# The up-projection's second half as rows: y of three token blocks made token by token, their gate logits as dot products on VectorE, and w_out's gated transpose in sixteen pieces

## The chip, the cores and the metric

The kernel runs on one core of one Trainium2 chip. The time is device microseconds of one launch; the span is the part of it that the profile covers.

## The reference

Three layers follow one another on 1536 tokens of 512 features:

```python
# 1: attention of 16 heads, keys masked by a 6-bit hash (head_dim 64, 768 tokens)
x = attention(q, k, v, proj)                       # (1536, 512)
# 2: one dense layer pair, called MoE1 here
h = x @ w_in                                       # 512 -> 2048
g = np.maximum(h, 0.0) + alpha * np.minimum(h, 0.0)
y = g @ w_out                                      # 2048 -> 512
# 3: eight experts, each with room for 192 tokens
logits = y @ w_gate                                # (1536, 8)
# the largest logit of all picks first, until every token has an expert with room
for e in range(8):
    out[mask_e] = np.maximum(y[mask_e] @ w1[e], 0.0) @ w2[e]
```

Since the choice of experts hangs on an order among 12288 logits, y and the logits are made to nearly fp32 accuracy: a product of two fp32 matrices is three fp32r products of their high and low parts.

## The kernel before

All is one instruction stream for each engine, written out by a planner (`Plan`): each operation (`op`) names the engines it may run on with a cost in us, a wished time `at`, what it follows, and which buffers it takes and gives back; a list scheduler then fixes engine and order. So a changed cost or wished time moves instructions everywhere, though they compute the same. The constants at the head of the file (`XP`, `RP`, `XA`, `RD`, ...) are such times.

In MoE1 the tokens are four blocks of 384 (blk 0 to 3) and the 2048 features are 16 groups f of 128.

- **h** (L699 to L701): for each f 12 fp32r products of 384 columns on TensorE (PE) into `psh`; then ScalarE (ACT) makes two parts (a1 L718, a2 L720), VectorE (DVE) joins them to `gt` (a3, L722), ACT takes the high part `gh` (L926), and DVE or GpSimd (POOL) the low part `gl` (`lo`, L930).
- **y** (L728 to L730): two feature groups later, 12 fp32r products of 384 columns for each f into `psy`. w_out is the stationary operand, so y comes out transposed: four banks of 128 features x 384 tokens.
- **End of a block** (blk 0 to 2): four copies `out` of y into `yt`; on PE four products with the gate matrix in column groups (`logit`, L798), a copy, three small products that add the groups (`pick`, L734), and four 128x128 transposes for each of three token groups t (`y_rows`, L777), whose rows `ysb` are stored to DRAM for the experts' gathers.
- **Block 3** takes its logits from g directly, with `wog` = w_out times w_gate, made while blocks 0 to 2 run (`wog_ops`): for each of four quarters q, four loads of w_out transposed, three DVE turns each that undo the 8-byte layout (L849, L851, L853), four products of 512 columns in four column groups (`prod`, L858), a copy, four small products (`add`, L866). Its h stage comes first; its y follows while the routing starts.
- **Conversions:** during block 0 w_out and the rest of w_in arrive as 8-byte numbers. DVE puts each piece together in three steps (L602, L605, L608), ACT takes the high part (L613), DVE the low part (L614). DVE also makes the low parts `xl` of the next block's input (L672), which may go to POOL where its op says so.
- **Experts:** h of an expert is `pl` (L1439), its output is split in 128 tokens (`oa`, L1471) and 64 tokens (`ob`, L1465); the gathered inputs are transposed by L1413 and L1414; routing's products (`rp`) lie between.

Of the kernel before, what the change touches and what calls it, by code (L numbers as in the profile page):

```python
# [7 lines left out]
F32 = mybir.dt.float32  # L8
# [16 lines left out]
XP = 10.89  # L25
RP = 11.53
RB = 19.57
PK0 = -119.54
PK = -106.32
# [8 lines left out]
WA = -6.05  # L38
XA = -32.34
TA = 20.0  # L40
TB = 1.5
YA = 0.74
RD = 2.82
# [4 lines left out]
IA = -7.85  # L48
# [480 lines left out]
class Moe:  # L529
    def __init__(s, tc, ctx, ident, w_in, w_out, w_out_t, alpha, w_gate, w1, w2, out):  # L530
        s.tc, s.nc, s.ident = tc, tc.nc, ident
        s.w_in, s.w_out, s.w_out_t, s.alpha, s.w_gate, s.w1, s.w2, s.out = w_in, w_out, w_out_t, alpha, w_gate, w1, w2, out
# [128 lines left out]
    def x_ops(s, pl, blk, k, after, at, w, take=()):  # L661
# [12 lines left out]
        o = pl.op({"ACT": 0.41}, hi, at, after, take)  # L674
        return pl.op({"DVE": 0.47, "POOL": 0.96} if blk else {"DVE": 0.47}, lambda e="DVE": lo(e), at + 0.4 * w, [o])
# [71 lines left out]
    def moe1(s, pl, r):  # L747
# [47 lines left out]
        def logit(blk):  # L795
            ps = T["lp", blk] = s.bank("pst", "OB")
            for k in range(4):
                nc.tensor.matmul(ps[32 * k:32 * k + 32, 0:NB], s.wg[:, k, :], T["yt", blk, k], start=True, stop=True)  # L798

# [4 lines left out]
        def logitp(blk):  # L804
            T["p2", blk] = s.bank("pst", "OB")
            s.pick(T["lt"], T["p2", blk])
# [7 lines left out]
        def y_after(blk):  # L814

            at = (blk * 16 + 15 + LAG) * U + 2.0
            o_o = []
# [20 lines left out]
        def wog_ops():  # L838
            raw = s.xT[:, :, 512:768].bitcast(U32)
            two = raw.rearrange("p a (n two) -> p a n two", two=2)  # L840
            src = s.w_out_t.rearrange("(p k) f -> k p f", k=4)

            def load(q, k):
                nc.sync.dma_start(out=raw, in_=src[k][:, q * 512:q * 512 + 512].bitcast(U32).rearrange("p (a n) -> p a n", a=4))

            def turn(k, n):
                t = s.xT[:, k, 0:512].bitcast(U32).rearrange("p (a n) -> p a n", a=4)
# [24 lines left out]
            for q in range(4):  # L872
                o_t = []
                for k in range(4):
                    at = (TA + (4 * q + k) * TB) * U
                    o_l = op({"SP": 0.45}, lambda q=q, k=k: load(q, k), at - 2 * U, o_x[1], ["RAW"], dma=1.46)
                    for n, t in enumerate((0.34, 0.6, 0.6)):
                        o_l = op({"DVE": t}, lambda k=k, n=n: turn(k, n), at + 0.1 * n, [o_l] + o, (), ["RAW"] if n == 2 else [])
                    o_t.append(o_l)
                a = op({"PE": 0.9}, prod, at + 0.5, o_t, ["OB"])  # L880
                a = op({"ACT": 0.5}, prodc, at + 0.6, [a], (), ["OB"])
                a = op({"PE": 0.8}, add, at + 0.7, [a], ["OB"])
# [13 lines left out]
        o_y, o_L, o_s, o_wog = {}, [], [], {}  # L896
# [3 lines left out]
        for blk in range(4):  # L900
            if blk < 3:
# [689 lines left out]
```

## Time and profile before

| | |
|---|---|
| median of 3 runs | 739.23 us (738.7 to 740.27) |
| profiled execution | 736.62 us |
| its span | 734.5 us |
| PE busy | 709.9 us, 97% of the span |
| DVE busy | 448.9 us, 61% |
| ACT busy | 311.3 us, 42% |
| POOL busy | 257.7 us, 35% |
| mean granted clock of PE | 0.991 |

The profiled execution took 2.1 us more than its span, and 2.6 us less than the median of the timed runs. Attention fills the first 226 us of the span; MoE1's blocks 0 to 2 end near 306, 380 and 454 us, block 3's h stage at 490, its y at 534; then come the experts to about 727 us and the last scatter.

### The profile page before, as it was taken

What the parts mean: (1) busy time and instruction counts of PE and PEld (TensorE: products, weight loads), DVE (VectorE), ACT (ScalarE), POOL (GpSimd) and SP (SyncE); (2) the same over time, 40 slices, a digit from 0 to 9 for tenths busy, and PEclk for the clock granted to TensorE, in tenths of its full rate; (3) what the DMA queues carried; (4) which work ended last, traced back from release to release, by engine and by line L of the source; (5) the groups of instructions that cost most, each with busy time, mean ns of one, the idle gap of its engine ahead of it and who ended that gap; (6) DMA issues with size and microseconds to landing.
All of it is one profiled execution on the core that took longest, in us unless ns stands there. A gap on an engine that the chain in (4) does not pass through costs nothing. (4 is left out here: it accounts for less than half of the span.)

```text
span 734.5 us, 14803 instructions
## 1 busy us (share of the span) xinstructions
PE 709.9 (97%) x6062; PEld 602.2 (82%) x6062; DVE 448.9 (61%) x989; ACT 311.3 (42%) x569; POOL 257.7 (35%) x220
## 2 busy tenths in 40 slices
PE   7999999999988799999999999999999999999996
PEld 6888888888887699999999999898978667666662
DVE  4888988888976989724454533456667565551000
ACT  4677787778743444633353333541021111112110
POOL 2498888889761121100000000005243413323101
PEclk9999999999999999999999999999999999999999
DMA  8455665655205455130223200200667546539201
GB/s 226 99 138 139 152 172 131 175 138 138 45 2 172 141 174 174 37 97 29 87 65 127 86 1 1 76 2 1 217 256 296 220 174 231 200 144 376 98 7 37
DMA packets 33091, 93.27 MB, mean 127 GB/s; under 512 B 4448, under 2 KB 17920, under 8 KB 30720
## 3 DMA queue, kind: packets, MB, share of 16 engines
q1 hardware_dynamic: 28016, 52.08, 24.8%
q0 software_dynamic: 4688, 39.85, 14.8%
q8 instruction: 48, 0.79, 0.4%
q10 hardware_dynamic: 320, 0.40, 0.2%
q14 instruction: 19, 0.16, 0.1%
HBM read 71.86 MB, written 8.65 MB: 110 GB/s over the span
## 5 line engine op out<-in xcount | busy, mean ns | idle before, releaser
L440 POOL TENSOR_TENSOR pl<-p 128x768 f16<-128x768 f32 (+1 forms) x94 | 134.5, 1449 | 35.6 <-ACT p L432 35.4
L334 DVE TENSOR_REDUCE m<-psm 128x1 bf16<-128x768 f32 x96 | 89.8, 956 | 13.9 <-PE psm L328 12.5
L432 ACT ACTIVATE p<-pss 128x768 f32<-128x768 f32 (+1 forms) x98 | 76.4, 797 | 40.2 <-PE pss L426 30.9
L699 PE MATMUL psh<-xh,win 128*128 128x384 f32 x256 | 87.9, 343 | 1.6 <-ACT xT L505 0.9
L701 PE MATMUL psh<-xh,win 128*128 128x384 f32 x256 | 85.9, 335 | 0.0
L700 PE MATMUL psh<-xl,win 128*128 128x384 f32 x256 | 85.7, 335 | 0.0
L930 POOL TENSOR_TENSOR gl<-gt,gh 128x384 fp32r<-128x384 f32 x18 | 19.1, 1066 | 171.4 <-ACT gh L926 169.7
L729 PE MATMUL psy<-gh,wout 128*128 128x384 f32 x192 | 65.2, 340 | 2.8 <-DVE wout L614 2.8
L728 PE MATMUL psy<-gl,wout 128*128 128x384 f32 x192 | 65.9, 343 | 2.0 <-ACT wout L613 2.0
L451 PE MATMUL av<-v,pl 128*128 128x65 f16 x576 | 63.5, 195 | 2.4 <-DVE xt L489 2.4
L730 PE MATMUL psy<-gh,wout 128*128 128x384 f32 x192 | 65.0, 338 | 0.0
L1471 PE MATMUL oa<-xw,ht 128*128 128x512 f32 x128 | 64.7, 598 | 0.0
L722 DVE SCALAR_TENSOR_TENSOR gt<-psh,al,gt 128x384 f32<-128x384 f32 x48 | 29.5, 615 | 55.4 <-ACT psh L720 55.3
L451 PEld LDWEIGHTS <-pl 128*128 128x128 f16 x576 | 53.9, 100 | 11.1 <-issue 11.0
L452 PE MATMUL av<-v,p 128*128 128x65 f16 x576 | 63.1, 195 | 0.0
L453 PE MATMUL av<-v,p 128*128 128x64 f16 x576 | 62.8, 195 | 0.0
L1439 PEld LDWEIGHTS pl<-xg,xw 128*128 128x128 f32 x256 | 42.1, 190 | 19.0 <-issue 18.2
L718 ACT ACTIVATE gt<-psh 128x384 f32<-128x384 f32 x48 | 23.6, 492 | 78.7 <-PE psh L701 78.7
L1439 PEld LDWEIGHTS pl<-xT,xw 128*128 128x128 f32 x256 | 41.9, 190 | 16.8 <-issue 14.6
L424 PE MATMUL pss<-Q,K 128*128 128x384 f32 x192 | 54.8, 364 | 0.9 <-ACT p L432 0.8
L699 PEld LDWEIGHTS psh<-xh,win 128*128 128x128 f32 x256 | 48.1, 188 | 8.2 <-issue 6.1
L452 PEld LDWEIGHTS <-p 128*128 128x128 bf16 x576 | 54.1, 99 | 0.1
(237 smaller groups left out, 1660.8 us busy)
## 6 DMA issues: line engine op xcount, KB each, us to landing
K<-Q SPq DMA_DIRECT2D x45, 192.0 KB, 2.9
wraw<-in_moe_w_out_dram SPq DMA_DIRECT2D x16, 512.0 KB, 3.6
xT<-in_moe_w_out_t_dram SPq DMA_DIRECT2D x16, 512.0 KB, 3.6
wraw<-in_moe_w_in_dram SPq DMA_DIRECT2D x12, 512.0 KB, 4.4
vf<-in_v_dram SPq DMA_DIRECT2D x16, 192.0 KB, 4.2
qk<-in_q_dram SPq DMA_DIRECT2D x15, 192.0 KB, 3.3
qk<-in_k_dram SPq DMA_DIRECT2D x15, 192.0 KB, 3.5
Q<-Q SPq DMA_DIRECT2D x15, 192.0 KB, 3.8
```

The costliest lines, as they stand in the source:

```text
L334: nc.vector.tensor_reduce(T["m"][:, t:t + 1], T["mx", t][:, :, 0:384], axis=AX.XY, op=OP.max, negate=True)
L432: nc.scalar.activation(T["p", c].rearrange("p (a n) -> p a n", a=2)[:, x], T["s", c][:, x, 0:384], AF.Exp, scale=0.125)
L440: (nc.vector if eng == "DVE" else nc.gpsimd).tensor_tensor(T["l", c][:, x], p[:, x], T["h", c][:, x], op=OP.subtract)
L451: nc.tensor.matmul(o[:, t, 0:65], lo[:, sl], vt[:, 0:65], start=(c == 0 and t == 0), stop=False, **kw)
L452: nc.tensor.matmul(o[:, t, 0:65], ph[:, sl], vt[:, 0:65], start=False, stop=False, **kw)
L699: nc.tensor.matmul(o, wl[:, k, ff], s.xh[blk][:, k], start=(k == 0), stop=False)
L700: nc.tensor.matmul(o, wh[:, k, ff], s.xl[blk][:, k], start=False, stop=False)
L701: nc.tensor.matmul(o, wh[:, k, ff], s.xh[blk][:, k], start=False, stop=(k == 3))
L728: nc.tensor.matmul(o, wh, gl, start=first, stop=False, skip_group_check=True)
L729: nc.tensor.matmul(o, wl, gh, start=False, stop=False, skip_group_check=True)
L730: nc.tensor.matmul(o, wh, gh, start=False, stop=last, skip_group_check=True)
L1439: nc.tensor.matmul(T["h", j // 2][:, j % 2], w1[:, k, j * 128:(j + 1) * 128], T["xg"][:, k], start=(k == 0 and j % 2 == 0), stop=(k == 3), ...
```

## The change

**y as rows.** In blocks 0 to 2 g is now the stationary operand: for each f and each 128 tokens t, three fp32r products with 512 columns of w_out (`yr`, `yr_mm`), 9 for each f and three banks instead of 12 and four. The rows are copied from `psy` to `ysb` and stored; `out`, `logit`, `pick` and `y_rows` are gone there.

**Logits.** For each row tile, 8 instructions on DVE (`dots`): ysb times a gate row broadcast over the partitions, with the sum taken into a column of `L` by the instruction's accumulator. There are 72, spread over the block that follows (`DA`). The gate rows come by three broadcast loads (`gate_rows`) behind the input of block 1 in `xT`'s room and in a tile of its own.

**wog.** The transposed w_out is handled in 16 pieces of 128 features instead of 4 quarters of 512 for each k: one load of all four k, the three turns, then `prod` with four products of 128 columns. The turns wait for a buffer `WT`; the first load waits for the input of block 2 instead of block 1, and a1 of block 3 stands behind the last piece.

**Planner.** Costs and wished times change with it, so that the order moves in all of MoE1 and the experts.

```diff
-XP = 10.89
...
-XA = -32.34
...
-RD = 2.82
+XP = 27.665
...
+XA = 60.587
...
+RD = 30.33
...
-        return pl.op({"DVE": 0.47, "POOL": 0.96} if blk else {"DVE": 0.47}, lambda e="DVE": lo(e), at + 0.4 * w, [o])
+        return pl.op({"DVE": 0.54, "POOL": 1.1} if blk else {"DVE": 0.54}, lambda e="DVE": lo(e), at + 0.4 * w, [o])
...
+    def yr_mm(s, o, f, t, gh, gl, first, last):
+
+        nc = s.nc
+        tt = slice(t * 128, t * 128 + 128)
+        wh, wl = s.wo_part(f, 0), s.wo_part(f, 1)
+        nc.tensor.matmul(o, gl[:, tt], wh, start=first, stop=False, skip_group_check=True)
+        nc.tensor.matmul(o, gh[:, tt], wl, start=False, stop=False, skip_group_check=True)
+        nc.tensor.matmul(o, gh[:, tt], wh, start=False, stop=last, skip_group_check=True)
...
-        def y_rows(blk, t):
-            T["p", blk, t] = s.bank("pst", "OB")
-            for k in range(4):
-                nc.tensor.transpose(T["p", blk, t][:, k * 128:(k + 1) * 128], T["yt", blk, k][:, t * 128:(t + 1) * 128], s.ident)
...
+            nc.sync.dma_start(out=d, in_=s.gate_t[:, e0 * 512:(e0 + n) * 512].to_broadcast([128, n * 512]).rearrange("p (e d) -> p e d", e=d.shape[1]))
...
-            any_copy(e, T["r", blk, t], T["p", blk, t])
+            any_copy(e, T["r", blk, t], T["y", blk, t])
+
+        def dots(blk, t, e):
+            like = lambda x: x.rearrange("p (a d) -> p a d", a=s.wgb[e].shape[1])
+            nc.vector.scalar_tensor_tensor(like(s.junk[:, 0:512]), like(T["r", blk, t]), 1.0, s.wgb[e], op0=OP.mult, op1=OP.mult,
+                                           accum_out=s.L[:, blk * 3 + t, e:e + 1])
...
-            for k in range(4):
-                o_o.append(op({"ACT": 0.37, "DVE": 0.47}, lambda e, k=k: out(e, blk, k), at, [o_y[blk, 15, k]], ["WR"] if k % 2 == 0 else [], ["L"],
-                              o_o[-1:]))
-            at += YA
-            o_l = op({"PE": 0.65}, lambda: logit(blk), at, o_o, ["OB"])
...
+                for e in range(8):
+                    o = op({"DVE": 0.78}, lambda t=t, e=e: dots(blk, t, e), at + DA * (8 * t + e), [o, o_gate[max(e // 2 - 1, 0)]], (), (["T"] + (["WR", "WR"] if blk == t == 2 else [])) if e == 7 else [], [a])
+                o_L.append(o)
...
-                for k in range(4):
-                    nc.tensor.matmul(T["wp"][32 * k:32 * k + 32], s.wg[:, k, :], s.xT[:, k, 0:512], start=True, stop=True)
+                    nc.tensor.matmul(T["wp"][32 * k:32 * k + 32, c * 128:c * 128 + 128], s.wg[:, k, :], w[:, k], start=True, stop=True)
...
-                o_gl = op({"DVE": 0.85, "POOL": 1.0}, lo, at + 1.3, [o], (), ["GT"] if b else [])
+                o_gl = op({"DVE": 0.55, "POOL": 1.1}, lo, at + 1.3, [o], (), ["GT"] if b else [])
...
-                        o_y[blk, f, k] = op({"PE": 0.49}, lambda blk=blk, f=f, k=k: y(blk, f, k), at + 0.1 * k,
+                        o_y[blk, f, t] = op({"PE": 0.68}, lambda blk=blk, f=f, t=t: yr(blk, f, t), at + 0.1 * t,
```

On PE, the end of a block before (here block 0, while block 1 begins): the rows from `pick` to the first transposes.

```order
L734 MATMUL pst<-c,lt 128x8 x3
L728 MATMUL psy<-gl,wout_4582 128x384
L729 MATMUL psy<-gh,wout_4582 128x384
L730 MATMUL psy<-gh,wout_4582 128x384
L728 MATMUL psy<-gl,wout_4582 128x384
L729 MATMUL psy<-gh,wout_4582 128x384
L730 MATMUL psy<-gh,wout_4582 128x384
L777 MATMUL pst<-c,yt 128x128 x4
```

The four gate products L798 stand seven rows ahead of these, and two more transposes L777 x4 behind, each after six products of 384 columns. In the changed kernel the last y products of block 0 (L738 to L740, w_out's last quarter) stand directly ahead of block 1's h (L700 to L702).

```order
L738 MATMUL psy<-wout_4585,gl 128x512
L739 MATMUL psy<-wout_4585,gh 128x512
L740 MATMUL psy<-wout_4585,gh 128x512
L700 MATMUL psh<-xh,win_76 128x384
L701 MATMUL psh<-xl,win_76 128x384
L702 MATMUL psh<-xh,win_76 128x384
L700 MATMUL psh<-xh,win_76 128x384
```

So nothing is left on PE between the blocks. On DVE, early in block 0 of the kernel before, the low parts of block 1's input (L672) stand ahead of the low part of w_out's second quarter (L614, `wout_4583`).

```order
L608 SCALAR_TENSOR_TENSOR pscv<-wraw,pscv 128x512
L672 TENSOR_TENSOR xl<-xT,xh 128x384
L602 TENSOR_SCALAR pscv<-wraw 128x512
L672 TENSOR_TENSOR xl<-xT,xh 128x384 x3
L614 TENSOR_TENSOR wout_4583<-pscv,wout_4583 128x512
```

The changed kernel has the same place without them; a low part of g (L954) stands two rows behind the L615 of that quarter, and one more stands further ahead.

```order
L609 SCALAR_TENSOR_TENSOR pscv<-wraw,pscv 128x512
L603 TENSOR_SCALAR pscv<-wraw 128x512
L723 SCALAR_TENSOR_TENSOR gt<-psh,al,gt 128x384
L615 TENSOR_TENSOR wout_4583<-pscv,wout_4583 128x512
L606 SCALAR_TENSOR_TENSOR pscv<-wraw,pscv 128x512
L954 TENSOR_TENSOR gl<-gt,gh 128x384
```

The four L672 of block 1 moved to POOL, and the low parts of g of some feature groups came from POOL to DVE. In block 3's h stage DVE now has dots (L805) between the a3 (L723) and the low parts (L954).

```order
L723 SCALAR_TENSOR_TENSOR xT<-psh,al,xT 128x384
L805 SCALAR_TENSOR_TENSOR junk,L<-ysb,wgb 128x512
L805 SCALAR_TENSOR_TENSOR junk,L<-ysb,xT 128x512
L954 TENSOR_TENSOR win_77<-xT,win_77 128x384
L723 SCALAR_TENSOR_TENSOR xT<-psh,al,xT 128x384
L805 SCALAR_TENSOR_TENSOR junk,L<-ysb,xT 128x512
L954 TENSOR_TENSOR win_78<-xT,win_78 128x384
```

The kernel before has only L722 and L930 there. On PE in the experts, before, the 64-token tails L1465 of expert 5 stand in parts between the h of expert 6 (L1439).

```order
L1465 MATMUL ob<-xw_5_8617,ht 64x512 x2
L1439 MATMUL pl<-xT,xw_6_8782 128x192 x7
L1465 MATMUL ob<-xw_5_8617,ht 64x512 x2
L1439 MATMUL pl<-xT,xw_6_8782 128x192 x3
L1471 MATMUL oa<-xw_5_8617,ht 128x512
L1439 MATMUL pl<-xT,xw_6_8782 128x192 x2
```

After, expert 5 stands in whole runs (h L1463, tails L1489, mains L1495).

```order
L1463 MATMUL pl<-xg,xw_5_8351 128x192 x30
L1489 MATMUL ob<-xw_5_8495,ht 64x512 x8
L1495 MATMUL oa<-xw_5_8495,ht 128x512 x8
L1437 MATMUL pl<-c,xT 128x128
L1438 MATMUL pl<-c,xT 128x128
```

Over all eight experts the 64 tail products stood in 26 runs, and stand in 12 now.

## Rows read from the trace of the kernel before

**Rows 1.** Windows by stage: busy us (instructions) of each engine, granted clock, DMA.
```profile
226.00:306.00 80.00, 74.49 (x413) 72.79 (x411) 70.64 (x117) 39.83 (x85) 16.66 (x16) 0.98 0.45 143
306.00:380.50 74.50, 74.50 (x451) 71.03 (x450) 32.58 (x59) 28.69 (x62) 1.24 (x1) 1.00 0.21 66
454.20:490.40 36.20, 36.20 (x228) 31.95 (x228) 19.12 (x43) 20.29 (x47) 1.07 (x1) 1.00 0.11 39
```

**Rows 2.** Timeline of PE, end of block 0: start, busy us, instruction.
```profile
305.77 0.34 PE L701 MATMUL psh<-xh,win 128*128 128x384 f32 x1
306.04 0.85 PE L798 MATMUL pst<-yt,wg 128*32 128x384 f32 x8
...
309.74 0.60 PE L777 MATMUL pst<-c,yt 128*128 128x128 f32 x4
...
314.22 0.34 PE L728 MATMUL psy<-gl,wout 128*128 128x384 f32 x1
...
316.31 0.34 PE L699 MATMUL psh<-xh,win 128*128 128x384 f32 x1
```

**Rows 3.** Timeline of PE, experts.
```profile
605.65 1.02 PE L1471 MATMUL oa<-xw,ht 128*128 128x512 f32 x2
606.50 0.49 PE L1439 MATMUL pl<-xg,xw 128*128 128x192 f32 x2
606.83 0.44 PE L1315 MATMUL rp<-tt,xT 128*128 128x2 f16 x12
```

**Rows 4.** Timeline of PE, one `prod` of `wog`, and a product in column groups of attention.
```profile
397.69 1.07 PE L858 MATMUL pswg<-xT,wg 128*32 128x512 f32 x8
398.69 0.45 PE L728 MATMUL psy<-gl,wout 128*128 128x384 f32 x1
398.97 0.34 PE L729 MATMUL psy<-gh,wout 128*128 128x384 f32 x1
...
69.58 0.53 PE L281 MATMUL psz<-qk,pz 128*32 128x192 f32 x8
70.05 0.62 PE L328 MATMUL psm<-K,Q 128*128 128x384 f32 x2
```

**Rows 5.** Timeline of PE, block 0, in brackets the idle time before.
```profile
255.05 0.41 PE L728 MATMUL psy<-gl,wout 128*128 128x384 f32 x1 [1.23 <-ACT wout L613]
257.50 0.66 PE L729 MATMUL psy<-gh,wout 128*128 128x384 f32 x1 [2.04 <-DVE wout L614]
...
258.27 0.52 PE L728 MATMUL psy<-gl,wout 128*128 128x384 f32 x1
258.59 0.52 PE L729 MATMUL psy<-gh,wout 128*128 128x384 f32 x1
```

**Rows 6.** Timeline of DVE, the same stretch.
```profile
255.34 1.50 DVE L672 TENSOR_TENSOR xl<-xT,xh 128x384 fp32r<-128x384 f32 x3
256.76 0.68 DVE L614 TENSOR_TENSOR wout<-pscv,wout 128x512 fp32r<-128x512 f32 x1
257.36 0.69 DVE L605 SCALAR_TENSOR_TENSOR pscv<-wraw,pscv 128x512 uint32<-128x512 uint32 x1
```

**Rows 7.** Timeline of PE, tails of one expert between the next expert's h.
```profile
694.68 1.08 PE L1465 MATMUL ob<-xw,ht 128*64 128x512 f32 x4
695.69 0.92 PE L1439 MATMUL pl<-xg,xw 128*128 128x192 f32 x4
696.53 1.08 PE L1465 MATMUL ob<-xw,ht 128*64 128x512 f32 x4
```

**Rows 8.** Timeline of DVE, attention: two fp32 sources in SBUF.
```profile
9.89 1.02 DVE L273 SCALAR_TENSOR_TENSOR K<-K,c,kk 128x768 fp32r<-128x768 f32 x1
10.83 1.01 DVE L273 SCALAR_TENSOR_TENSOR Q<-Q,c,qq 128x768 fp32r<-128x768 f32 x1
```

**Rows 9.** Timeline of ACT, attention: an accumulator read.
```profile
16.65 0.19 ACT L365 ACTIVATION_READ_ACCUMULATOR vabs<-vf 128x1 f32 x1
16.87 0.53 ACT L365 ACTIVATE vabs<-vf 128x384 bf16<-128x384 f32 x1
```

More of the change, by code (lines that the diff above doesn't have):

```diff
@@ L24 @@
 XWAIT = 0.0005
-XP = 10.89
[L26 to L29, printed above, removed]
+XP = 27.665
+RP = 3.994
+RB = 52.305
+PK0 = 38.012
+PK = 16.878
 NPL = 4
@@ L37 @@
 LAG = 2
-WA = -6.05
-XA = -32.34
-TA = 20.0
-TB = 1.5
-YA = 0.74
-RD = 2.82
+WA = -4.451
+XA = 60.587
+TA = 22.847
+DA = 4.774
+TB = 1.087
+YA = -3.908
+RD = 30.33
 HC = 1
@@ L529, with __init__ @@
 class Moe:
-    def __init__(s, tc, ctx, ident, w_in, w_out, w_out_t, alpha, w_gate, w1, w2, out):
+    def __init__(s, tc, ctx, ident, w_in, w_out, w_out_t, gate_t, alpha, w_gate, w1, w2, out):
         s.tc, s.nc, s.ident = tc, tc.nc, ident
-        s.w_in, s.w_out, s.w_out_t, s.alpha, s.w_gate, s.w1, s.w2, s.out = w_in, w_out, w_out_t, alpha, w_gate, w1, w2, out
+        s.w_in, s.w_out, s.w_out_t, s.gate_t, s.alpha, s.w_gate, s.w1, s.w2, s.out = w_in, w_out, w_out_t, gate_t, alpha, w_gate, w1, w2, out
         s.ctx = ctx
@@ L672, in lo @@
             (nc.vector if e == "DVE" else nc.gpsimd).tensor_tensor(s.xl[blk][:, k], s.xT[:, k, n], s.xh[blk][:, k].bitcast(F32), op=OP.subtract)
-        o = pl.op({"ACT": 0.41}, hi, at, after, take)
-        return pl.op({"DVE": 0.47, "POOL": 0.96} if blk else {"DVE": 0.47}, lambda e="DVE": lo(e), at + 0.4 * w, [o])
+        o = pl.op({"ACT": 0.5}, hi, at, after, take)
+        return pl.op({"DVE": 0.54, "POOL": 1.1} if blk else {"DVE": 0.54}, lambda e="DVE": lo(e), at + 0.4 * w, [o])
     def x_init(s, cl):
@@ L802, in logitc, with yr @@
             any_copy(e, T["lt"], x()[:, 0:NB])
-        def logitp(blk):
-            T["p2", blk] = s.bank("pst", "OB")
-            s.pick(T["lt"], T["p2", blk])
+        def yr(blk, f, t):
+            if f == 0:
+                T["y", blk, t] = s.bank("psy", "L")
+            g = s.g[blk, f]
+            s.yr_mm(T["y", blk, t], f, t, g[1], g[2], f == 0, f == 15)
         def y(blk, f, k):
@@ L838, in wog_ops, with load, turn @@
         def wog_ops():
-            raw = s.xT[:, :, 512:768].bitcast(U32)
+            raw = s.xT[:, :, 768:1024].bitcast(U32)
             two = raw.rearrange("p a (n two) -> p a n two", two=2)
[L841 to L847, printed above, removed]
+            w = s.xT[:, :, 1024:1152]
+            src = s.w_out_t.rearrange("(p k) f -> p k f", k=4)
+            def load(q, c):
+                f = (4 * q + c) * 128
+                nc.sync.dma_start(out=raw, in_=src[:, :, f:f + 128].bitcast(U32))
+            def turn(n):
+                t = w.bitcast(U32)
                 if n == 0:
@@ L875, in wog_ops @@
                     at = (TA + (4 * q + k) * TB) * U
[L876 to L882, printed above, removed]
+                    o_l = op({"SP": 0.45}, lambda q=q, k=k: load(q, k), at - 2 * U, o_x[2], ["RAW"], dma=1.46)
+                    for n, t in enumerate((0.45, 0.7, 0.75)):
+                        o_l = op({"DVE": t}, lambda n=n: turn(n), at + 0.1 * n, [o_l], ["WT"] if n == 0 else [], ["RAW"] if n == 2 else [])
+                    o_t.append(op({"PE": 0.35}, lambda k=k: prod(k), at + 0.5, [o_l], ["OB"] if k == 0 else [], ["WT"]))
+                o_wt.extend(o_t)
+                a = op({"ACT": 0.5}, prodc, at + 0.6, o_t, ["T"], ["OB"])
+                a = op({"PE": 0.8}, add, at + 0.7, [a], ["OB"], ["T"])
                 o = [op({"DVE": 0.1}, lambda q=q: addc(q), at + 0.8, [a], (), ["OB"])]
@@ L894, in sel @@
             s.pick(T["lt"], s.p, False)
-        o_y, o_L, o_s, o_wog = {}, [], [], {}
+        o_y, o_L, o_s, o_wog, o_wt = {}, [], [], {}, []
+        s.wgb = {}
+        o_x[1] = x_block(1)
+        o_x1 = o_x[1]
+        o_gate = [op({"SP": 0.6}, lambda i=i: gate_rows(i), 8 * U, o_x1, (), dma=3.2 - 1.6 * i) for i in range(2)]
+        o_gate.append(op({"SP": 0.6}, lambda: gate_rows(2), 12 * U, (), ["WR", "WR"], behind=[o_w[15]], dma=1.6))
         o_h = []
@@ L900, in moe1 @@
         for blk in range(4):
-            if blk < 3:
+            if blk < 3 and blk + 1 not in o_x:
                 o_x[blk + 1] = x_block(blk + 1)
@@ L1525, in body @@
     ident = c[:, 0:128]
-    m = Moe(tc, ctx, ident, w_in, w_out, w_out_t, alpha, w_gate, w1, w2, out)
+    m = Moe(tc, ctx, ident, w_in, w_out, w_out_t, gate_t, alpha, w_gate, w1, w2, out)
     m.sel = c[:, 260:268]
```

65 lines of the change are left out of this document (36 added, 29 removed).

## The prediction

> **What bounds it now.** I read the windows by stage first: from 226 us on PE is busy in nearly all of each stage, 74.5 of 74.5 us in block 1 [rows 1]. So in MoE1 and the experts an edit is worth what it takes off PE, unless another engine then comes late. Two stages have another engine near: in block 0 DVE is busy 70.6 of 80 us, and PE idles 5.5 us; in block 3's h stage DVE is busy 19.1 of 36.2 us [rows 1]. In block 1 DVE has some 40 us free, and block 2 repeats it. The timelines then give what each removed, added or moved piece costs on PE, and in block 0 what it waits for. Time is accounted against the profiled run, 736.6 us (2.1 us above its span, 2.6 us under the median).
>
> **Ends of blocks.** From the L701 at 305.77 to the L728 at 314.22 there are 8.45 us, with 31 products of 384 columns in them [rows 2]. Twelve such products, from 314.22 to 316.31, take 2.09 us, so 0.174 each [rows 2], and 31 take 5.40. The 3.05 us left are the logit, pick and three transposes with their edges. They go in three blocks, on PE, which is the path: **-9.1 us**. The row copies stay, reading `psy` instead of `pst`; two of three banks must be free when the next block's y begins, over 4 us of h later, so they cost nothing.
>
> **y as rows.** 192 products of 384 columns take 33.4 us a block. 144 products of 512 do the same columns in fewer instructions, and no row has that form. Bounds: if time goes by columns alone, 0.174 x 512/384 = 0.232 us each, 33.4 us, no gain. At the other end, L1471 needs 0.85 us for two records of 512 columns, 0.427 each [rows 3]; L1439's record of 192 takes 0.165 [rows 3], 0.86 ns a column against 0.45 for fp32r, so a record is about two fp32r passes and a pass of 512 takes 0.214: 30.8 us, -2.6 a block, -7.8 in all. Between them: at the low clock the y product takes 0.32 us (258.27 to 258.59) [rows 5], at the high one 0.174; a part that doubles with the clock (0.146) and one that does not (0.028) give 0.195 + 0.028 = 0.223 us for 512. That is also the middle, and I take it: 144 x 0.223 = 32.1, -1.3 a block, **-3.9 us** (0 to -7.8).
>
> **wog in pieces.** A `prod` of four 512-column products takes 1.00 us to the next product, and four of 192 columns in column groups 0.47 [rows 4]. On a line through both, 128 columns take 0.15 + 0.21 = 0.36 us. The product behind takes 0.1 more than its 0.174 (398.69 to 398.97 [rows 4]), and I give the edge ahead as much, so 0.2 for both: 4 x 1.20 = 4.8 before, 16 x 0.56 = 9.0 after, **+4.2 us**. Lower bound +3.2 (edges do not repeat wholly), upper +5.5 (all of 0.47 plus edges). The turns have the same elements on DVE, now in blocks 1 and 2, where it has room; a late turn would hold PE at a piece, but the pieces are spread over two blocks.
>
> **Block 0.** PE idles 1.23 us for ACT's high part of w_out and then 2.04 us for DVE's low part (L614) [rows 5]. DVE is not idle: ahead of that L614 stand three xl, 1.42 us from 255.34 to 256.76, 0.47 each, and one more before [rows 6]. The four go to POOL, 1.9 us off DVE; one a3 and one low part more come ahead of this L614, about 1.0. What is late next is the conversion itself: it comes 0.9 us earlier. PE also ran at half its clock after the wait, at 0.32 instead of 0.174 us a product [rows 5], for eleven products: 1.6 us. With a shorter wait that may or may not happen, so I count half: **-1.7 us**. Bounds 0 (another piece of the chain is as late) and -4.9 (both waits and the low clock go). POOL has room (16.7 of 80 us busy [rows 1]) for the four.
>
> **Experts.** Four tail records of 64 tokens take 1.01 us to the next h [rows 7], where four passes of 0.214 would be 0.86; the four records of h behind them take 0.84 [rows 7] instead of 4 x 0.165 = 0.66. A change to the 64-row form and back thus costs about 0.35 us. The order has 26 such runs before and 12 after: 14 x 0.35 = **-4.9 us** (0 if the cost sits in the instructions, not in the change).
> Whole runs of one expert leave PE nothing to do between its h and its output where ht, a gather or a weight is late. Before, the mains of the expert before lay there. I take **+1.0 us** for such waits (0 to 3 in the likeliest case).
>
> **The dots.** 72 instructions of 128x512 with two fp32 sources in SBUF and an accumulator, DVE only. No row has all of this. DVE starts a 512-element instruction every 0.60 us (256.76 to 257.36) [rows 6]; two fp32 SBUF sources of 768 elements take 0.94 us (9.89 to 10.83) [rows 8], no slower per element; the one accumulator read in rows is ACT's, 0.22 us (16.65 to 16.87) [rows 9]. So 0.60 to 0.82 us; I take 0.78, nearer the upper, since each also waits for the one before. In blocks 1 and 2 24 x 0.78 = 19 us hide in 40 us of room. The tight place is block 3's h stage, where the a3 frees the bank of h: 36.2 us less 3.0 of block end is 33.2 us. DVE's 19.1 us in 43 instructions [rows 1] hold about 0.08 each of overlap (busy 0.68, next start after 0.60 [rows 6]), so 15.7 us of occupancy; one row copy goes from it, but 0.6 us pass before the first dot has its row. That leaves 33.2 - 15.7 - 0.6 = 16.9 us. Two of the 24 dots stand behind the last a3; 22 x 0.78 = 17.2, 0.3 us too long; since a3s also fall behind a dot now and then, I add 0.9: **+1.2 us** (0 at 0.60, +2.0 at 0.82).
> The DMAs are three broadcast loads, 2 MB, behind the conversion's loads, and sixteen of w_out transposed as before; block 1 moves 66 GB/s at a DMA share of 0.21 [rows 1], so they are hidden.
>
> **Sum.** -9.1 - 3.9 + 4.2 - 1.7 - 4.9 + 1.0 + 1.2 = -13.2 us: 723.4 us for the profiled run, 726.0 for the median.
>
> **Rivals.**
> 1. *DVE paces block 3 (slower).* If a dot with an accumulator runs at half the rate of a plain instruction, its 512 elements take twice the 0.94 x 512/768 = 0.63 us, 1.25, and with an accumulator read of 0.22, 1.47 us. Then 22 x 1.47 - 16.9 + 0.9 = 16.3 us are lost in block 3 instead of 1.2: -13.2 - 1.2 + 16.3 = +1.9, 741.1 us. It eats the whole gain (14.4 without this term) from 0.04 us less, d = 1.38. Against it: rows 8's full rate with two such sources. For it: no row has the accumulator. The Trainium skill, "Vector Engine (DVE) Microarchitecture Reference", "Points that are easy to get wrong", says that this instruction with two non-bf16 SBUF sources runs at half throughput, both read ports being taken and none left for the accumulator's readback. By that rule the trace disagrees for the form without an accumulator (0.94 us for 768), and no run here shows the form with one. Chance 0.08.
> 2. *The experts take it back.* Each of eight changes of expert, and the routing phases that now stand denser in the first half, wait 1 to 2 us for ht, a gather or weights: 10 us more, 736 us (731 to 740). For it: PE has at most two banks of h ahead and no mains to fill in. Against it: h of one expert comes in eight chunks, so only the last one's ht is new when the tails begin, and the mains stand behind the tails. Chance 0.13.
> 3. *Cheap rows.* The 512-column product takes 0.214 us: 3.9 us more gain, 722.1 us. For it: L1471's records carry almost no fixed part [rows 3]. The Trainium skill, "TensorE: Matmul & The Clock Gate", gives N/2.4 + 2.5 ns for the isolated gap, 216 ns at N = 512; by that y would come to 144 x 0.216 = 31.1 us a block, -6.9 in all, where 384 columns by the same rule would be 0.1625 and the trace has 0.174. Chance 0.15.
> 4. *Grouping and block 0 give nothing* (-6.6 missing): 732.6 us. The form's cost would have to sit in the instruction, which the slower h records behind a tail [rows 7] speak against. Chance 0.10, inside the range.
>
> **From chances to numbers.** The forecast as summed has 0.54 (723 to 730), rivals as given. The range from 721 to 737 leaves out rival 1, the upper part of rival 2 and the outer edge of rival 3, about 0.17. 0.2% (1.5 us) is what a measurement of this kernel can tell. Faster by more: all but rival 1 and a quarter of rival 2, and a rest for a mechanism not seen: 0.86; within: 0.06; slower: 0.08.
>
> **What would show it.** Right: PE without a gap at 306, 380 and 454 us, L738 to L740 starting every 0.223 us, L805 every 0.6 to 0.8 us, PE's wait for L615 near 256 us shorter, and tails at 0.22 us a record. Wrong: waits of h (L700) for a3 (L723) in block 3's stage over 2 us; low clock in a stage that had none; waits at L1489 or L1463 for ht or xg; pieces L876 waiting for their turns. The weakest terms are the form of the y product, since no row has it, and the experts' order.

## The result, and the profile after

The changed kernel took 727.87 us (median of 4, 725.68 to 728.81) beside 739.75 before: 0.9841 of the time before, 95% interval 0.9813 to 0.9869. A second set of runs gave 725.57 us and 0.9847 (0.9825 to 0.9869). So some 11.5 us are gone; 13.2 were forecast, 726.0 us for the median.

The windows by stage of the changed kernel (first profile; columns as in [rows 1]), cut at the first h of MoE1, the ends of the three blocks, the first y product behind block 3's h and the first h of the experts:

```profile
226.59:305.27 78.68, 75.31 (x360) 67.21 (x361) 67.24 (x110) 38.58 (x80) 13.16 (x13) 0.96 0.47 151
305.27:377.12 71.85, 71.85 (x401) 62.05 (x399) 50.18 (x108) 26.19 (x57) 3.83 (x3) 1.00 0.24 79
377.12:451.00 73.88, 73.88 (x425) 63.47 (x425) 48.57 (x101) 24.44 (x54) 7.58 (x6) 1.00 0.24 78
451.00:486.33 35.33, 35.33 (x218) 31.82 (x216) 30.23 (x80) 19.98 (x46) 4.11 (x7) 1.00 0.10 37
486.33:529.74 43.41, 42.15 (x340) 38.67 (x339) 30.42 (x111) 5.11 (x12) 17.79 (x17) 1.00 0.28 93
529.74:727.00 197.26, 189.82 (x1185) 131.83 (x1182) 84.08 (x321) 31.00 (x61) 53.92 (x47) 0.99 0.51 190
```

In blocks 1 to 3 PE is busy all the time: DVE went from 32 to 50 us in block 1 [rows 1] and from 19 to 30 in block 3's h stage, and PE waits for it nowhere there. The second profile has the same lengths but for block 0:

```profile
225.13:301.14 76.01, 72.50 (x361) 64.54 (x361) 67.19 (x110) 38.54 (x80) 13.19 (x13) 1.00 0.48 157
```

The 2.7 us between the two are the granted clock at the start of MoE1. In the first profile of the changed kernel (timeline of PE) the first 18 products start 0.32 us apart, until 232.4 us: the granted clock is 0.5 there, the lower of TensorE's two levels, after PE had waited 1.83 and 0.90 us at attention's end.

```profile
227.08 0.53 PE L701 MATMUL psh<-xl,win 128*128 128x384 f32 x1
227.40 0.53 PE L702 MATMUL psh<-xh,win 128*128 128x384 f32 x1
```

in the second one 0.17 us apart:

```profile
225.42 0.34 PE L701 MATMUL psh<-xl,win 128*128 128x384 f32 x1
225.59 0.33 PE L702 MATMUL psh<-xh,win 128*128 128x384 f32 x1
```

This low clock falls in some executions of the changed kernel and of the edited forms of the kernel before, and not in others, so a stage's length is compared below between profiles alike in it. By the timelines, from the start of a stage's first product to that of the next stage's, in us ("early" is a low clock at MoE1's start; block 3 is its h stage, y(3) what follows it):

| profile | early | block 0 | block 1 | block 2 | block 3 | y(3) | experts to end |
|---|---|---|---|---|---|---|---|
| before | no | 79.25 | 74.02 | 74.05 | 36.90 | 44.06 | 200.74 |
| changed, first | yes | 78.45 | 71.85 | 73.88 | 34.80 | 44.17 | 197.26 |
| changed, second | no | 75.78 | 71.85 | 73.88 | 34.79 | 44.18 | 197.29 |
| second less before | | -3.5 | -2.2 | -0.2 | -2.1 | +0.1 | -3.4 |

(The first four columns go from last y to last y, block 3's to its last h.) That adds up to -11.3 us, and -0.3 in attention, which no instruction of PE changed: the span of 734.5 fell to 722.9. The first profile of the changed kernel, 727.0, understates the change because of its early low clock. The kernel before has a low clock too, in the middle of block 0: eleven products behind its wait of 2.04 us [rows 5], about 1.6 us, where the changed kernel has none. So of the -3.5 us in block 0, 2.0 are waits of PE (5.5 us before, 3.5 after) and 1.6 are this clock.

Blocks 1, 2 and 3 differ so much because the pieces of wog do not stand evenly: seven are in block 1 and nine in block 2, and one of the four `add` (0.8 us and its edges) moved from block 1 to block 3's h stage.

The timeline of PE at the end of block 0, first profile of the changed kernel, where [rows 2] had 3.05 us of logit, pick and transposes:

```profile
305.04 0.40 PE L740 MATMUL psy<-wout,gh 128*128 128x512 f32 x1
305.27 0.34 PE L700 MATMUL psh<-xh,win 128*128 128x384 f32 x1
...
307.38 0.40 PE L738 MATMUL psy<-wout,gl 128*128 128x512 f32 x1
307.62 0.40 PE L739 MATMUL psy<-wout,gh 128*128 128x512 f32 x1
...
311.58 0.40 PE L738 MATMUL psy<-wout,gl 128*128 128x512 f32 x1
...
313.67 0.34 PE L700 MATMUL psh<-xh,win 128*128 128x384 f32 x1
```

Nothing stands between the blocks any more. But from 311.58 to 313.67 nine row products take 2.09 us, 0.233 each: to the hundredth what the twelve took before [rows 2]. y as rows gave PE nothing by itself.

A piece of wog (same view): from 326.04 to 327.01 there are 0.97 us; less 0.233 for the y product and 0.175 for the h product, 0.56, as forecast.

```profile
326.04 0.40 PE L740 MATMUL psy<-wout,gh 128*128 128x512 f32 x1
326.37 0.43 PE L876 MATMUL pswg<-xT,wg 128*32 128x128 f32 x8
326.73 0.44 PE L700 MATMUL psh<-xh,win 128*128 128x384 f32 x1
327.01 0.34 PE L701 MATMUL psh<-xl,win 128*128 128x384 f32 x1
```

The dots on DVE (timeline of DVE, first profile):

```profile
306.38 0.69 DVE L805 SCALAR_TENSOR_TENSOR junk<-ysb,xT 128x512 f32<-128x512 f32 x1
306.99 0.08 DVE L805 DVE_READ_ACCUMULATOR junk<-ysb,xT 128x1 f32 x1
307.10 1.38 DVE L805 SCALAR_TENSOR_TENSOR junk<-ysb,xT 128x512 f32<-128x512 f32 x1
308.41 0.08 DVE L805 DVE_READ_ACCUMULATOR junk<-ysb,xT 128x1 f32 x1
```

A dot takes 0.72 us to the next dot (306.38 to 307.10), its accumulator's read included, and 0.61 to that read: the full rate of [rows 6]. The Trainium skill, "Vector Engine (DVE) Microarchitecture Reference", "Points that are easy to get wrong", says that this instruction with two SBUF sources that are not bf16 runs at half throughput; this trace disagrees. The dot of 1.38 us is another matter (last section). And the tails, in a whole run (timeline of PE, second profile): 16 records in 3.58 us, 0.224 each, where four in a part took 1.01 and the h behind them 0.2 more than its own [rows 7].

```profile
705.09 3.65 PE L1489 MATMUL ob<-xw,ht 128*64 128x512 f32 x16
708.67 7.13 PE L1495 MATMUL oa<-xw,ht 128*128 128x512 f32 x16
```

### The profile page after: what moved, and what is told of

It reads as the page before. It is cut to its first block, busy times and chain, and to the rows that moved or that the text cites. A ratio compares the mean times of both kernels' runs of the same rounds, so it can differ in the third digit from the quotient of the medians.

```text
span 727.0 us, 14706 instructions
## 1 busy us (share of the span) xinstructions
PE 704.0 (97%) x5936; PEld 582.0 (80%) x5936; DVE 496.5 (68%) x1125; ACT 304.4 (42%) x553; POOL 265.7 (37%) x226
## 4 chain that ended last, share of the span: by engine, by line
PE 88%; DVE 5%; issue 2%; DMA 2%; POOL 1%; ACT 1%; ACTq 0%; POOLq 0%; DVEq 0%
PE pl L1463 12%; PE oa L1495 7%; PE psh L700 6%; PE psh L702 6%; PE psh L701 6%; PE pss L425 5%; PE psm L329 5%; PE psy L738 4%; PE pss L427 4%; PE psy L740 4%; PE psy L739 4%; PE ob L1489 4%; PE av L452 3%; PE av L454 2%; PE av L453 2%
## 5 line engine op out<-in xcount | busy, mean ns | idle before, releaser
L335 DVE TENSOR_REDUCE m<-psm 128x1 bf16<-128x768 f32 x96 | 89.8, 956 | 14.7 <-PE psm L329 13.2
L700 PE MATMUL psh<-xh,win 128*128 128x384 f32 x256 | 89.3, 349 | 4.3 <-DVE gt L723 3.4
L702 PE MATMUL psh<-xh,win 128*128 128x384 f32 x256 | 87.3, 341 | 0.0
L701 PE MATMUL psh<-xl,win 128*128 128x384 f32 x256 | 87.3, 341 | 0.0
L1495 PE MATMUL oa<-xw,ht 128*128 128x512 f32 x128 | 59.6, 609 | 0.0
L700 PEld LDWEIGHTS psh<-xh,win 128*128 128x128 f32 x256 | 49.0, 191 | 12.0 <-DVE gt L723 4.8
L738 PE MATMUL psy<-wout,gl 128*128 128x512 f32 x144 | 57.2, 397 | 0.0
L740 PE MATMUL psy<-wout,gh 128*128 128x512 f32 x144 | 57.0, 396 | 0.0
L739 PE MATMUL psy<-wout,gh 128*128 128x512 f32 x144 | 56.9, 395 | 0.0
L723 DVE SCALAR_TENSOR_TENSOR gt<-psh,al,gt 128x384 f32<-128x384 f32 x48 | 29.5, 615 | 39.7 <-ACT psh L721 39.6
L453 PEld LDWEIGHTS <-p 128*128 128x128 bf16 x576 | 54.1, 99 | 0.1
L454 PEld LDWEIGHTS <-p 128*128 128x128 bf16 x576 | 54.1, 99 | 0.0
L329 PE MATMUL psm<-K,Q 128*128 128x384 f32 x192 | 51.1, 360 | 0.5 <-DVE Q L355 0.4
L954 POOL TENSOR_TENSOR gl<-gt,gh 128x384 fp32r<-128x384 f32 x12 | 13.3, 1106 | 104.7 <-ACT gh L950 99.0
```

Source lines behind the costliest of these rows:

```text
L329: nc.tensor.matmul(T["mx", t][:, a, 0:384], T["Q1"].rearrange("p a n -> p (a n)")[:, t * 128:(t + 1) * 128], T["K1"][:, a], start=True, st ...
L335: nc.vector.tensor_reduce(T["m"][:, t:t + 1], T["mx", t][:, :, 0:384], axis=AX.XY, op=OP.max, negate=True)
L453: nc.tensor.matmul(o[:, t, 0:65], ph[:, sl], vt[:, 0:65], start=False, stop=False, **kw)
L454: nc.tensor.matmul(o[:, t, 0:64], ph[:, sl], vt[:, 66:130], start=False, stop=(c == 5 and t == 5), **kw)
L700: nc.tensor.matmul(o, wl[:, k, ff], s.xh[blk][:, k], start=(k == 0), stop=False)
L701: nc.tensor.matmul(o, wh[:, k, ff], s.xl[blk][:, k], start=False, stop=False)
```

## The experiments

The theory after the result: the change is a sum of PE time, block ends -9.1, pieces +4.2, tails some -3.5, and a block 0 in which DVE is less late, with nothing for the rows' form and nothing for the dots. The rivals: tails cost nothing by their grouping, the dots are tight, block 0's gain is the clock's.

**The changed kernel again.** No edit.

> The changed kernel once more, for a second profile and a closer ratio. If the change is worth what the stages of the two profiles add up to (block 0 -0.7, block 1 -2.2, block 2 -0.2, block 3's h -2.2, experts -3.5, so -8.6 from the first h of MoE1 on), then the ratio is near 0.988, and the stages have these lengths again within 0.5 us. If the -11.9 of the medians is the change's own, the ratio stays near 0.984 and a stage, most likely attention's end or block 0, is shorter here by 2 to 4 us than in the first profile of the changed kernel.

0.9847 (0.9825 to 0.9869), and block 0 shorter by 2.7 us, the rest within 0.03: the second case. The loss of the first profile was the clock's.

**Tails: the order alone, both ways.** In the kernel before, and the reverse in the changed one:

```diff
-XP = 10.89
-RP = 11.53
-RB = 19.57
-PK0 = -119.54
-PK = -106.32
+XP = 27.665
+RP = 3.994
+RB = 52.305
+PK0 = 38.012
+PK = 16.878
```

> The kernel before with five of the planner's constants (XP, RP, RB, PK0, PK) taken from the changed one: 15 runs of tails instead of 26, the rest as before. If the change of form costs 0.35 us each, 11 x 0.35 = 3.9 us faster, 0.995 of before. If grouping costs or gives nothing by itself, 0.999 to 1.001. If whole runs make PE wait for ht or gathers, PE's idle time in the experts grows by the difference.

> The changed kernel with the five constants of before: 26 runs of tails again, rows, dots and pieces as changed. If grouping is an additive term, 14 x 0.35 = 4.9 us less whatever whole runs cost in waits: 3.5 to 4.9 us slower than the changed kernel, and what is left against before is MoE1's part, -5 us (0.993). If the gain of the change sits in MoE1, it stays within 1 us of the changed kernel.

The kernel before with the new order: 0.997 (0.9948 to 0.9992), 2.2 us faster. The windows of its y(3) and experts are

```profile
490.92:535.48 44.56, 42.97 (x346) 1.00 0.28 92
535.48:733.20 197.72, 190.72 (x1182) 0.99 0.50 189
```

-3.0 us in the experts for 11 runs fewer, 0.27 each, and +0.5 in y(3), where PE's waits name a copy of y (`psr` L972, 0.6 us). The changed kernel with the old order: 0.9954 (0.9935 to 0.9973), so some 8 us slower than the changed kernel by the two ratios, 6.6 by the spans of two profiles, with

```profile
481.88:526.79 44.91, 43.12 (x343) 1.00 0.27 85
526.79:729.50 202.71, 194.69 (x1184) 0.99 0.50 186
```

that is +5.4 us in the experts and +0.7 in y(3), above the 4.9 of the additive case. 1.4 us of the 5.4 are waits for gathers and copies of gathered rows that this mixture has. So the order is worth 3 to 4 us in itself, and the changed kernel's -3.4 is that. The five constants move all of the experts' order and not only the tails, but PE's timelines show where the time sits. Summed from each product's start to the next one's start, less idle time, the h products take 89.9 us in the kernel before and 86.7 with the new order, the tails 31.5 and 30.5, the mains (L1471) 55.3 and 56.5. The changed kernel has 86.5, 29.6 and 56.6, and with the old order 90.6, 31.6 and 55.3: the gain is in the tails and in the h beside them, and 1.3 us of it are lost again in the mains.

**Dots twice.** `dots` issues its instruction two times.

```diff
-            nc.vector.scalar_tensor_tensor(...)
+            for _ in range(2):
+                nc.vector.scalar_tensor_tensor(...)
```

> Each dot is issued twice, with the same result. The rows of the changed kernel show 0.60 to 0.73 us a dot, so a pair takes 1.2 to 1.45. By the prediction's account of block 3 (16.9 us of room on DVE for 22 dots) 22 x 1.33 - 16.9 + 0.9 = 13.3 us are lost there, and blocks 1 and 2 lose nothing (48 dots of 0.67 = 32 us a block beside 50 us busy less 16 of the single dots = 66 of 72 to 74 us): 741 us, slower than the changed kernel by 1.8%. Rival: the room is larger, since dots may trail behind the last a3 while y of block 3 runs on PE; then the loss is under 5 us and DVE never was the tight place.

1.0324 (1.0289 to 1.0359), 762.5 us: much worse than either case. Blocks 1 and 2 took 84.87 and 87.60 us, 13.0 and 13.7 more, block 3's h stage only 7.5 more, y(3) 3.1. The window of block 1 and PE's waits in blocks 1 and 2:

```profile
304.80:389.67 84.87, 75.38 (x401) 64.48 (x400) 66.04 (x156) 25.48 (x57) 3.86 (x3) 0.96 0.20 67
PE pswg L886 <- ACT wc L881: 6.5, 1, 6.5
PE psy L738 <- DVE gl L955: 6.1, 3, 2.2
PE pswg L877 <- DVE xT L871: 5.6, 2, 3.1
```

DVE has 66 us of work in 85 us, as I had added it up, and yet PE waits: for low parts and turns that stand behind dots in DVE's queue, and for ACT, whose row copies wait 7.1 us, and whose copy `wc` waits 0.8, for a row buffer that the dots still hold. PE's waits are 18.2 of the 26.7 us that blocks 1 and 2 lost. The other 8.5 are PE's own work taking longer: the granted clock falls to its lower level in three stretches there, 20.5 us in all, each during one of the waits or just behind it (0.96 of full clock in block 1, 0.92 in block 2). Busy time against the stage's length was the wrong test of room; the order within the queue decides. Single dots leave enough slack for every one of these, double ones don't.

**Rows in halves.** `yr_mm` makes two products of 256 columns instead of one of 512. The two halves share a bank, and their sums do not come out right in it (why, no run here shows), so y of blocks 0 to 2, and with it which expert gets which token, is not the reference's. The number of products and their columns are as said.

```diff
-        nc.tensor.matmul(o, gl[:, tt], wh, ...)
+        for c in (slice(0, 256), slice(256, 512)):
+            nc.tensor.matmul(o[:, c], gl[:, tt], wh[:, c], ...)
```

> The changed kernel with every product of 512 columns as two of 256, the same columns in 288 instead of 144 products a block. The changed kernel's rows show 0.233 us for 512 columns beside 0.174 for 384, the same per column. If time goes by columns alone, 256 take 0.116 us and the time stays (725.6, within 0.3%). If a fixed part of 28 ns sits in each product, as the prediction took it, 144 x 0.028 = 4 us a block, 12 us slower. If loading the stationary operand bounds a short product, 256 columns take more than 0.12 us, up to 0.16, and the time rises by up to 3 x 288 x 0.045 = 39 us.

731.36 us, 0.9894 (0.9856 to 0.9931); blocks 1 and 2 grew by 0.7 us each. Timeline of PE:

```profile
380.72 0.28 PE L739 MATMUL psy<-wout,gl 128*128 128x256 f32 x1
380.84 0.28 PE L740 MATMUL psy<-wout,gh 128*128 128x256 f32 x1
...
381.44 0.33 PE L700 MATMUL psh<-xh,win 128*128 128x384 f32 x1
```

Six products take 0.72 us, 0.12 each, beside 0.174 for 384 and 0.233 for 512: about 0.44 ns a column and 6 ns fixed. The 28 ns that I took from the two clocks is not there: by it a block would have grown by 4 us, and 0.7 us for 144 more products are 5 ns each.

**Block 0's low parts of g on POOL**, in the changed kernel:

```diff
-                    (nc.vector if e == "DVE" else nc.gpsimd).tensor_tensor(g[2], ...)
+                    (nc.vector if e == "DVE" and blk else nc.gpsimd).tensor_tensor(g[2], ...)
```

> The changed kernel with all low parts of g of block 0 on POOL instead of some 8 of them on DVE. In the changed kernel PE's waits in block 0 are all for the a3 on DVE, 3.5 us. If DVE's queue is what is late, eight times 0.48 us less on it shorten these waits by 2 to 3.5 us: block 0 from 75.8 to about 73 us, 0.981 of before. Rival: POOL takes 1.0 us for each and brings y late, or the a3 is late for another reason (ACT's parts), and block 0 stays within 0.5 us.

0.9832 (0.9802 to 0.9862), not to be told from the changed kernel. PE still waits, in block 0:

```profile
PE psh L700 <- DVE gt L723: 3.7, 4, 1.1
```

Block 0 took 77.69 us (early low clock; 78.45 in the first profile). It has 12 products at the early low clock where that first profile has 18, which is 0.9 us, so block 0 gained nothing. The eight lows are there, but only one of them (229.69 us in the second profile) stands ahead of the last of these waits, the next at 255.83 behind it.

What the a3 is late for can be read in that second profile (timelines of ACT, DVE and PE, the third of the four waits):

```profile
248.71 0.49 ACT L721 ACTIVATE psh<-psh 128x384 f32<-128x384 f32 x1
251.20 0.61 DVE L723 SCALAR_TENSOR_TENSOR gt<-psh,al,gt 128x384 f32<-128x384 f32 x1
251.87 0.45 PE L700 MATMUL psh<-xh,win 128*128 128x384 f32 x1 [0.85 <-DVE gt L723]
```

ACT's part was ready at 249.20, 2.0 us before the a3 starts; between them DVE works on conversion steps. At the other three waits it is 1.0 to 2.1 us, each more than PE's wait, and DVE has no gap from 228.48 to 257.81 us. So it is DVE's queue, with the conversion in it, and not ACT.

**All low parts of blocks 1 to 3 on DVE**, and block 2's input too.

```diff
+                    (nc.vector if e == "DVE" or blk else nc.gpsimd).tensor_tensor(g[2], ...)
```

> The changed kernel with the low parts of blocks 1 to 3, and those of block 2's input, on DVE instead of POOL. In the changed kernel six dots take 1.3 to 1.5 us instead of 0.68, each while POOL runs a TENSOR_TENSOR. If the two hold each other up, no dot takes over 0.9 us here, apart from those beside block 1's input on POOL. If the long dots come from elsewhere (a late row, a broken record), some stay. The stages keep their lengths within 0.5 us either way, since DVE has room.

All stages as in the second profile within 0.2 us. Lines of DVE from 300 to 500 us, where the changed kernel's first profile has means of 754 and 723 ns for the two:

```profile
L805 DVE SCALAR_TENSOR_TENSOR junk<-ysb,xT 128x512 f32<-128x512 f32 x54 | 37.0, 686 | 4.9 <-ACT ysb L770 4.3
L805 DVE SCALAR_TENSOR_TENSOR junk<-ysb,wgb 128x512 f32<-128x512 f32 x18 | 12.3, 685 | 0.1
```

The long dots are gone, as the first case had it.

**Block 0 of the kernel before, by parts.** First block 1's x lows on POOL, then wog's loads behind block 2's input (so that the turns leave block 0), then both.

```diff
-            (nc.vector if e == "DVE" else nc.gpsimd).tensor_tensor(s.xl[blk][:, k], ...)
+            (nc.vector if e == "DVE" and blk != 1 else nc.gpsimd).tensor_tensor(s.xl[blk][:, k], ...)
```

```diff
-                    o_l = op({"SP": 0.45}, lambda q=q, k=k: load(q, k), at - 2 * U, o_x[1], ["RAW"], dma=1.46)
+                    o_l = op({"SP": 0.45}, lambda q=q, k=k: load(q, k), at - 2 * U, o_x[2], ["RAW"], dma=1.46)
```

> The kernel before with the four low parts of block 1's input on POOL, nothing else changed. They stand on DVE ahead of the low part of w_out for which PE waits 2.04 us. If they are what is late, the wait shrinks by 1.4 to 1.9 us, and if the low clock behind it came from the wait, 1.6 us more go: block 0's stage from 79.3 to about 75.8 us, 0.995 of before. If the low clock stays, -1.9 us (0.9975). If the next conversion step is as late, nothing (1.000).

> The kernel before with the loads for wog behind block 2's input instead of block 1's, so that its turns stand on DVE in blocks 1 and 2 and no longer in block 0, the x lows as before. In the kernel before a turn stands directly ahead of three of the low parts of w_out, but behind the waits of PE. If only what stands ahead of the 2.04 us wait counts, block 0 stays at 79.3 us (80.7 when the low clock falls at MoE1's start).

> The kernel before with both: block 1's x lows on POOL and wog's turns out of block 0. With the x lows alone the 2.04 us wait shrank to 0.23, but 1.18 and 0.69 us came later, where turns stand ahead of a low part of w_out: block 0 gained nothing. If DVE's queue as a whole is late and both relieve it, these later waits go too: block 0 1.9 to 3.5 us shorter (75.8 to 77.4; 78.4 when the low clock falls at MoE1's start), which would be the changed kernel's whole gain there. If the later waits stay, it is the conversion itself, and the gain in block 0 has another cause than these two.

The x lows alone: 0.9982 (0.9959 to 1.0004), block 0 80.75 us with an early low clock, where the run without transposes below, alike in block 0, had 80.69. Each of the two has 16 products at that clock and none at it later. The wait of 2.04 us is gone, but PE, being earlier, waits later (timeline of PE, waits alone):

```profile
259.31 0.44 PE L729 MATMUL psy<-gh,wout 128*128 128x384 f32 x1 [0.23 <-DVE wout L614]
262.69 0.46 PE L699 MATMUL psh<-xh,win 128*128 128x384 f32 x1 [1.18 <-DVE gt L722]
268.03 0.45 PE L729 MATMUL psy<-gh,wout 128*128 128x384 f32 x1 [0.69 <-DVE wout L614]
```

The turns alone: 738.86 us in a single run, the 2.04 us wait as before, block 0 81.43. This profile has the early low clock and a second one behind that wait, which the 80.69 lacks, so the two lengths can't be compared; PE's waits are 5.2 us beside 5.4. Both: 0.9986 (0.9965 to 1.0007), block 0 79.49, 1.2 us less than the 80.69, and of the later waits one is left:

```profile
262.45 0.44 PE L699 MATMUL psh<-xh,win 128*128 128x384 f32 x1 [1.14 <-DVE gt L722]
```

The lengths mix waits and clock: the early low clock has 14 products here, 16 in the 80.69 and 18 in the changed kernel's 78.45, 0.15 us each. PE's waits in block 0 are the cleaner measure: 5.4 us without either, 4.6 with both, 3.4 in the changed kernel. So the two are 0.8 of its 2.0 us. The wait that is left comes from elsewhere (timeline of DVE, both):

```profile
261.19 0.69 DVE L602 TENSOR_SCALAR pscv<-wraw 128x512 uint32<-128x512 uint32 x1 [0.81 <-DMA wraw<-in_moe_w_out_dram]
261.80 0.60 DVE L722 SCALAR_TENSOR_TENSOR gt<-psh,al,gt 128x384 f32<-128x384 f32 x1
```

DVE, being earlier, now waits for the load of a piece of w_out, with the a3 right behind it. In neither the kernel before nor the changed one does DVE wait for that load; what in the new order keeps it from that, I did not take apart.

**Pieces in pairs**, in the changed kernel: a second room for a turned piece, and one `prod` for two.

```diff
+            w = lambda c: s.junk[:, 512:1024].rearrange("p (k n) -> p k n", k=4) if c % 2 else s.xT[:, :, 1024:1152]
...
+                for d in (c - 1, c):
+                    for k in range(4):
+                        nc.tensor.matmul(T["wp"][32 * k:32 * k + 32, d * 128:d * 128 + 128], s.wg[:, k, :], w(d)[:, k], start=True, stop=True)
```

> The changed kernel with a second room for a turned piece of w_out (the unused half of the dots' output tile), so that the products of two pieces stand together on PE: 8 times 8 products instead of 16 times 4. In the changed kernel's rows a piece costs 0.56 us, of which some 0.2 us are the edges and 0.15 us the fixed part of the line through the two rows of before. If these are paid once for each group, 8 x 0.2 = 1.6 to 8 x 0.35 = 2.8 us less, all in blocks 1 and 2: 0.981 to 0.9825 of before, faster than the changed kernel. Rival: the edges belong to each piece's operands, and the stages stay within 0.3 us; or the dots now wait for PE's reading of their output tile, and blocks 1 and 2 grow.

0.9828 (0.9795 to 0.986), 726.01 us: faster than before, but not to be told from the changed kernel by the runs. By the stages blocks 1 to 3 lost 1.5, 0.2 and 0.8 us, 2.5 in all, and y(3), whose products begin earlier among the last h here, another 0.8 that I did not take apart. Timeline of PE:

```profile
331.04 0.42 PE L877 MATMUL pswg<-xT,wg 128*32 128x128 f32 x8
331.28 0.40 PE L877 MATMUL pswg<-junk,wg 128*32 128x128 f32 x8
331.61 0.44 PE L700 MATMUL psh<-xh,win 128*128 128x384 f32 x1
```

The second piece of a pair adds 0.24 us instead of 0.56: 8 x 0.32 = 2.6, what the stages show. This profile had the early low clock (78.12 in block 0) and 1.0 us more in the experts, where PE waits 0.7 us for gathered rows beside 0.2 and the granted clock is 0.95 in the last 44 us beside 0.97 in the first profile of the changed kernel.

**The kernel before without transposes.**

```diff
-            T["p", blk, t] = s.bank("pst", "OB")
-            for k in range(4):
-                nc.tensor.transpose(T["p", blk, t][:, k * 128:(k + 1) * 128], T["yt", blk, k][:, t * 128:(t + 1) * 128], s.ident)
+            T["p", blk, t] = T["yt", blk].rearrange("p a n -> p (a n)")[:, 0:512]
```

> The kernel before without the transposes at the ends of blocks 0 to 2: the row copies read 512 elements of the transposed y as they lie, so the rows that are stored are not y's, and what the experts gather is wrong; the rest is as before. If the end of a block costs PE what its rows show, three transposes are 3 x 0.45 = 1.3 us: blocks 1 and 2 from last y to last y 1.3 us shorter (72.7 instead of 74.0), block 3's h stage too. If the copies behind them, or the banks, are what costs, the stages shrink by less than 0.7 us.

Its windows of blocks 1 and 2:

```profile
305.98:378.64 72.66, 72.66 (x431) 69.61 (x431) 31.80 (x58) 28.69 (x62) 1.24 (x1) 1.00 0.24 70
378.64:451.37 72.73, 72.73 (x432) 69.68 (x432) 29.90 (x53) 25.12 (x54) 1.24 (x1) 1.00 0.21 63
```

1.36, 1.32 and 1.38 us less in blocks 1, 2 and 3, as the rows priced it: the transposes are PE time, nothing hides them. The other 1.7 us of an end of block, the logit and `pick` with their edges, no run took alone; that they are PE time too is read from the rows.

## Why the prediction was right, and where it was not

The direction, the size of the sum and the range held. One term promised too much (y as rows), two too little (block 0, the dots).

- **Ends of blocks, -9.1: held.** Nothing is left in the rows after, and taking the transposes alone gave 1.35 of the 3.05 us a block. **Pieces, +4.2: held**, 0.56 us each. Together -4.9 in blocks 1 to 3; the stages lost 4.45, and 0.3 of the 0.45 us between are the row products of blocks 1 and 2 (144 x 0.233 = 33.55 us a block beside 33.4). The upper bound for the pieces was misadded: 0.47 and 0.2 of edges for each of 16 would be +5.9, not +5.5.
- **y as rows, -3.9: wrong, nothing.** The step that failed is the split of 0.174 us into "a part that doubles with the clock (0.146) and one that does not (0.028)". The product at full clock costs by its columns, 0.453 ns each at 384 and 0.455 at 512, though a column at the low clock takes 0.83 ns, less than twice that. So a product at the low clock, 0.32 us, doesn't tell a fixed part of one at the high clock; why it takes less than twice the time stays open. The bound that I named first, "0.174 x 512/384 = 0.232 us", was the result. Rival 3 fell with it: the row product takes 0.233 us, not 0.214. The Trainium skill, "TensorE: Matmul & The Clock Gate", "Back-to-back issue gap", gives 216 ns for the isolated gap at 512 columns; the rows show 233 for fp32r.
- **Block 0, -1.7: right in place, short in size,** -3.5 between profiles without an early low clock, -2.2 between such with one. The conversion was to come 0.9 us earlier; the waits fell by 2.0, from 5.5 to 3.5 us, and are all for the a3 now. The low clock behind the wait, counted at half of 1.6 us, is in the profile of the kernel before in full and is gone in full after; in the pair with an early low clock neither side has it. The reason that I gave, the four x lows, is only part of it: alone they moved the wait, as the run shows, and gained nothing; with the turns they are 0.8 of the 2.0.
- **Experts, -4.9 + 1.0: held as a net,** -3.4. Tails and h gained 5.3 us, near the 4.9. The +1.0 was luck: it was meant for waits, and those are 0.3 us (rival 2 fell with them); what cost 1.3 us were the mains, which I had left alone.
- **Dots, +1.2: nothing.** PE waits for no DVE instruction from the end of block 0 to the end of block 3's h. The price was within its bounds, 0.72 us to the next dot where I took 0.78; with 0.72 my own sum gives nothing, and rival 1's half rate fell. But the reckoning of room was wrong: at twice the price 37 us are lost, not the 16 that it gives, and most of it in blocks 1 and 2, which I had called free. Rival 1's break-even, d = 1.38, is 0.09 us under its 1.47, not 0.04.

That the sum came out close, -13.2 for -11.5, is partly luck: y as rows missed by about 4 us one way, the dots (1.2) and block 0 (0.5 to 1.8) made up for 1.7 to 3.0 of it the other way.

## What to carry to other kernels

Merging fp32r products of the same columns into fewer, longer ones gave PE nothing here; changing which operand is stationary paid because it made transposes and a second product unnecessary at a serial place. Small groups of products in another tile form paid their edges each time here (0.3 to 0.4 us a run of tails, 0.32 a piece): keep them together. Room on an engine is not the stage's length less its busy time: look at what stands behind the new instructions in its queue, and try them twice.

## What the runs showed of the hardware

A dot and a POOL instruction hold each other up. The dot of 1.38 us above, twice a dot's 0.68, started while POOL ran this one (timeline of POOL, first profile of the changed kernel):

```profile
306.36 1.57 POOL L673 TENSOR_TENSOR xl<-xT,xh 128x384 fp32r<-128x384 f32 x1 [7.66 <-ACT xh L670]
```

Each of the six dots of over 1.3 us overlaps such an instruction of POOL, and with these on DVE none is left; POOL's own takes 1.57 us here, where others of its kind take 1.01. The Trainium skill, "SBUF — State Buffer", "SBUF: two separate sides", says that a DVE instruction with two SBUF inputs and a GpSimd instruction that reads SBUF take turns at a shared pair of ports, one being held off until the other ends; the trace agrees within 0.13 us: the dot ends 0.55 us after POOL's 307.93, and takes 0.68 alone. It cost nothing in time here.

The low clock of attention's end falls in MoE1's first products in some executions only, 0.32 instead of 0.174 us a product for 12 to 18 of them; with 18, block 0 is 2.7 us longer in the changed kernel.
